# Measured durations in the planner of a fused attention, routing and two-layer kernel, and four buffers for an output tile

## The chip, the cores and the metric

The kernel runs on one core of one Trainium2 chip. The metric is the device time of one execution in microseconds; three runs of the kernel before gave 895.02 (median), 894.41 and 896.03.

## The reference

Three parts follow each other, all in float32:

```python
# 1: retention-like attention, 4 batches x 8 heads x 576 positions x 64
scores = q @ k.T / sqrt(64)
x = (scores * Dmat) @ v            # Dmat[i, j] = gamma_h ** (i - j) for i >= j, else 0
x = x.transpose(0, 2, 1, 3).reshape(2304, 512)
# 2: tokens to 8 experts, at most 2304 / 8 = 288 each, greedily by logit
order = argsort(-(x @ w_gate).flatten())
for idx in order:                  # the highest (token, expert) pair first
    tok, e = idx // 8, idx % 8
    if assigned[tok] >= 0 or counts[e] >= 288: continue
    assigned[tok] = e; counts[e] += 1
out[mask_e] = relu(x[mask_e] @ w1[e]) @ w2[e]     # 512 -> 1024 -> 512
# 3: a dense layer, 512 -> 2048 -> 512
h = out @ w_in;  g = h * tanh(softplus(h));  y = g @ w_out
```

The weights w_in and w_out arrive as 64-bit floats and are narrowed to 32 bits on the chip.

## The kernel before, in words

`attention` computes part 1 tile by tile (18 tiles of 128 tokens). It writes x to a scratch tensor in HBM and keeps the logits. In the same loop 17 of the 32 pieces of w_in and w_out are narrowed (`EARLY = 17`); this is the early narrowing of the kernel. It fills about the first 118 us.

Everything after that is a set of Python generators, started in `moe` (line 877). Each `yield` names an engine, a cost in nanoseconds, the events it comes after, and a priority (lower goes first). `run_tasks` (line 694) is a list scheduler: it holds a planned time per engine, adds 200 ns (`HOP`) for each event, picks the task that can start first (a more urgent one of the same engine goes before it when it could start soon enough), advances the engine's planned time by the cost, and lets the generator emit its instructions. The order of emission is the order of each engine's queue on the chip. The costs are never part of the program: they set only that order. On the chip every engine works off its queue strictly in order and waits for semaphores, so an instruction planned too early holds up all that is behind it.

The generators are these:

- `route` (line 403) finds one expert after the other that fills up: eight rounds. A round takes six steps by a digit of the threshold: VectorE compares (tile G), TensorE counts with 18 small matmuls (pF), VectorE compares the counts (sat), TensorE spreads the digit (pD). Then VectorE marks the tokens (over, scan) and TensorE makes prefix sums (pP). Its priority is 0.
- `tokens` (line 598, priority -1) makes the list of 288 tokens of a group: VectorE compares positions in two halves (ohb), TensorE sums (pI), VectorE makes idx, POOL issues three indirect DMAs which gather rows of x into xg (three of 96 rows of 2 KB), and twelve transposes on TensorE (mmx, line 661) turn them. ScalarE and VectorE split the result into a high and a low float32r part (xh, xl).
- `weights_of` and `unit` load the eight 512 KB units of an expert's weights through SyncE into three stage buffers (st). `split_unit` (line 580) splits each into high and low parts: ScalarE makes whi, POOL or VectorE makes wlo.
- `experts` (line 797, priority 2) runs the products of the experts: per expert 96 matmuls for the first layer (mma, line 784) and 96 for the second (mmb), three for each exact product (high-high, low-high, high-low). ScalarE and VectorE make hh and hl from mma, and ScalarE copies mmb to y, which SyncE stores to HBM. Five PSUM banks go round among mma, mmb, mmx and pI.
- `narrow` (line 732) takes the remaining 15 pieces of w_in and w_out: ScalarE, VectorE (dw, lines 756 and 763) and POOL or VectorE, priority 4, or 1.5 when it falls behind a pace in planned time.
- `tiles` runs the last layer: 96 hidden tiles (mmc), each with a gate of reciprocals and products on VectorE, ScalarE and POOL, and the outer products (po). It begins when the last expert's first layer is done.

The function `result` (line 814) makes y. It asks for the event of the second last store, since there are two buffers:

```python
at = yield ACT, 290, [at, *self.stored[-2:-1]], 0
y = self.fa.tile([P, CAP], F32, name="y", bufs=2)
```

Of the kernel before, what the change touches and what calls it, by code (L numbers as in the profile page):

```python
# [7 lines left out]
F32 = mybir.dt.float32  # L8
# [9 lines left out]
P = 128  # L18
# [6 lines left out]
CAP = N // E  # L25
# [9 lines left out]
NRING = 12  # L35
CLOSED = -1.0e37
# [6 lines left out]
GATHER = 2200  # L43
# [9 lines left out]
EID = -2  # L53
# [79 lines left out]
class Kernel:  # L133
# [267 lines left out]
    def route(self):  # L401
# [8 lines left out]
        for i in range(E):  # L410
# [21 lines left out]
            if i:  # L432
                at = yield DVE, 210, [at], 0
                key = self.at("key")
                v.scalar_tensor_tensor(key, self.dead, CLOSED, raw, op0=ALU.mult, op1=ALU.add)
            known = None
            for s in range(6):
                m = WIDTHS[s]
                if s or i:
                    at = yield DVE, m * 20 + (0, 950, 420, 420, 420, 420)[s], [at], 0  # L440
# [20 lines left out]
                    if s:  # L461
                        side = yield DVE, 300, [at], 0
# [11 lines left out]
                    at = yield PE, 475, [at], 0  # L474
# [3 lines left out]
                    at = yield DVE, 75, [at], 0  # L478
                    sat = self.saturated(pF, m)
                at = yield PE, 20, [at], 0  # L480
                pD = self.psum("pD", [P, E])
                nc.tensor.matmul(pD, self.digit[:m, s, :], sat[:m], start=True, stop=True)
            at = yield DVE, 1400, [at], 0
# [20 lines left out]
            marked = yield PE, 60, [at], 0  # L504
# [12 lines left out]
            at = yield DVE, 900, [marked, at], 0  # L517
# [30 lines left out]
    def weights_of(self, junk, at):  # L548
# [5 lines left out]
        at = yield DVE, 80, [at], EID  # L554
# [24 lines left out]
    def split_unit(self, n, st, at, eng, into, prio):  # L579
# [7 lines left out]
        hi = yield ACT, 950, [at, *before, *place], prio  # L587
# [3 lines left out]
        lo = yield ({POOL: 2310, DVE: 1140} if eng is None else eng), 1140, [hi], prio  # L591
# [4 lines left out]
    def tokens(self, i, pos, at):  # L596
# [4 lines left out]
        at = yield DVE, 600, [at], pr  # L601
# [6 lines left out]
        side = yield DVE, 500, [at], pr  # L608
# [8 lines left out]
        for ts in halves:  # L617
            ready.append((yield DVE, 525, [at], pr))
            v.tensor_tensor(ohb[:, ts], bb[:, ts, None].to_broadcast([P, NT // 2, GB]), self.rc[:, None, RC["slot"]].to_broadcast([P, NT // 2, GB]), op=ALU.is_equal)  # L619
        pI = None  # L620
        for ts, made in zip(halves, ready):
            at = yield PE, 490, [made, side, *([] if pI is not None else [self.bank])], pr
            if pI is None:
                nI, pI = self.take_bank(f"pI{i}")
                pI = pI[:GB, :6]
            for t in range(ts.start, ts.stop):
                nc.tensor.matmul(pI, ohb[:, t], R[:, t].rearrange("p g c -> p (g c)"), start=(t == 0), stop=(t == NT - 1))
        at = yield DVE, 75, [at], pr
# [3 lines left out]
        self.banks[nI] = at  # L632
        if i > 1:
            yield None, 0, [lambda: self.gathered.get(i - 2)], pr
        at = yield POOL, 3100, [at], pr
# [13 lines left out]
        def rest(c, n, pT, at):  # L649
            hi = yield ACT, 290, [at], pr  # L650
            nc.scalar.copy(xh[:, c], pT[:, :CAP])
            ready = yield DVE, 370, [hi], pr
# [32 lines left out]
    def free(self, n):  # L685

        last = [self.banks[j - 5] if len(self.banks) >= 5 - j else Event(0) for j in range(n)]
        return None if None in last else max(last, key=lambda e: e.t)

# [42 lines left out]
    def narrow(self):  # L732
# [16 lines left out]
        def piece(n, st, now, dst):  # L749
            now = yield ACT, 520, [now, *at("turn", n - 1), *at("sign", n - 2)], self.narrow_priority  # L750
# [3 lines left out]
            now = yield DVE, 400, [now, *at("shift", n - 1), *at("store", n - 3)], self.narrow_priority  # L754
# [3 lines left out]
            sign = yield ACT, 520, [now], self.narrow_priority  # L758
            nc.scalar.sign(t, st[:, :, 1].bitcast(F32))
            for c in range(0, 512, 512 // PARTS):  # L760
                cs = slice(c, c + 512 // PARTS)
                now = yield DVE, 665 if PARTS == 1 else 365, [now], self.narrow_priority
                v.scalar_tensor_tensor(w[:, cs], st[:, cs, 0], ic[:, IC["low"]], w[:, cs], op0=ALU.logical_shift_right, op1=ALU.bitwise_or)
            done["read"][n] = max(sign, now, key=lambda e: e.t)
            now = yield {POOL: 1230, DVE: 600}, 0, [now, sign], self.narrow_priority
# [10 lines left out]
    def product(self, name, terms, first=True, last=True, bank=None):  # L776

        n = len(terms)
        for j, term in enumerate(terms):
            for h in range(3):  # L780
                at = yield PE, 123, [lambda: (term() or (0, None))[1], *([] if bank else [self.bank])], 2
# [15 lines left out]
    def experts(self):  # L797
        nc, a = self.nc, self.a
        for i in range(E):
# [3 lines left out]
            def rest(f, bank, at):  # L803
                hi = yield ACT, 290, [at], 0
# [3 lines left out]
                ready = yield DVE, 370, [hi], 2  # L808
# [5 lines left out]
            def result(i, d, bank, at):  # L814
                at = yield ACT, 290, [at, *self.stored[-2:-1]], 0
                y = self.fa.tile([P, CAP], F32, name="y", bufs=2)
# [60 lines left out]
    def moe(self):  # L877
# [15 lines left out]
        self.freed, self.banks, self.stored, self.narrowed = [], [], [], {}  # L893
        self.loaded, self.rounded, self.staged = {}, {}, {}
        self.layer1, self.gathered, self.features = {}, {}, {}
# [213 lines left out]
```

## Time and profile before

| what | us |
|---|---|
| median of three runs | 895.02 |
| the profiled execution | 903.27 |
| its span, first to last instruction | 901.5 |
| TensorE busy | 818.8 (91%) |
| VectorE busy | 699.5 (78%) |
| ScalarE busy | 411.4 (46%) |
| POOL busy | 464.4 (52%) |
| mean granted TensorE clock | 0.933 |

The profile comes from one execution on the chip. A busy time is the sum over the stretches in which the engine executed something. The granted clock is 1.0 when TensorE runs at 2.4 GHz and 0.5 when it runs at 1.2 GHz. A wait is put down to the instruction whose semaphore came last. In the timeline, the bracket behind a row is the idle time of the engine before that row and what ended it.

### The profile page before, as it was taken

The page shows a single profiled execution, that of the slowest core. Times are in us where ns is not written, and L with a number is a line of the kernel's source. Part 1 is how long each engine was busy: PE and PEld are TensorE (multiplying, and loading weights), DVE is VectorE, ACT ScalarE, POOL GpSimd, SP SyncE. Part 2 cuts the span into 40 slices and gives each one's busy share as a digit, 9 for nine tenths or more (in the row PEclk, how much of TensorE's full clock was granted, in tenths as well). Part 3 has the DMA queues.
Part 4 walks back from the last instruction along what each step waited for, and adds up shares of the span by engine and source line. Part 5 has one row for each costly group of instructions (what it writes and reads, how often), then busy time and mean ns, then how long its engine had stood idle before and what let it go on. Part 6 is the DMA issues. An engine that isn't in the chain of part 4 may idle for free.

```text
span 901.5 us, 15523 instructions
## 1 busy us (share of the span) xinstructions
PE 818.8 (91%) x5821; PEld 736.1 (82%) x5821; DVE 699.5 (78%) x1110; ACT 411.4 (46%) x736; POOL 464.4 (52%) x400
## 2 busy tenths in 40 slices
PE   7899864989898989877999988999999999999997
PEld 5788742878787878767999977998999899899995
DVE  4367665687576757766538999999899899899894
ACT  0244421434243434343538544655655655645543
POOL 4466401565655747531003765766655655755644
PEclk9899858788987988988999999999999999999999
DMA  9999736376756768576558010100100100100000
GB/s 345 346 372 371 226 138 143 118 141 213 165 161 160 194 160 160 175 200 169 166 161 270 32 36 1 53 19 0 53 19 1 54 18 1 59 12 1 36 1 36
DMA packets 66331, 112.37 MB, mean 125 GB/s; under 512 B 10192, under 2 KB 38224, under 8 KB 66256
## 3 DMA queue, kind: packets, MB, share of 16 engines
q1 hardware_dynamic: 63280, 101.94, 36.5%
q0 software_dynamic: 2976, 9.44, 5.1%
q8 instruction: 46, 0.75, 0.4%
q14 instruction: 29, 0.24, 0.1%
HBM read 88.81 MB, written 22.55 MB: 124 GB/s over the span
## 4 chain that ended last, share of the span: by engine, by line
PE 51%; DVE 24%; DMA 15%; issue 5%; POOL 3%; ACT 2%; SPq 0%; POOLq 0%; DVEq 0%; ACTq 0%
PE mmc L988 15%; PE po L1049 15%; PE mmb L784 6%; DVE q L1018 5%; DMA xg<-x_scratch,idx 5%; PE mma L784 4%; DVE n L1013 3%; DMA st<-w 2%; PE pF L477 2%; DMA w_out<-dw 2%; DVE ohb L619 2%; DMA st<-w_in 2%; DMA mask<-masks 2%; PE pL L244 2%; PE pA L203 1%
## 5 line engine op out<-in xcount | busy, mean ns | idle before, releaser
L1018 DVE RECIPROCAL q<-q 128x384 f32<-128x384 f32 x96 | 244.1, 2543 | 11.6 <-ACT q L1016 10.5
L592 POOL TENSOR_TENSOR wlo<-st,whi 128x1024 fp32r<-128x1024 f32 x50 | 120.2, 2416 | 153.2 <-ACT whi L589 141.4
L1020 POOL TENSOR_TENSOR n<-n,q 128x384 f32<-128x384 f32 x96 | 99.9, 1040 | 106.4 <-DVE q L1018 102.2
L988 PE MATMUL mmc<-yl,whi 128*128 128x384 f32 x384 | 130.2, 339 | 3.4 <-POOL yl L948 2.9
L988 PE MATMUL mmc<-yh,whi 128*128 128x384 f32 x384 | 130.0, 339 | 2.6 <-DVE n L1023 2.6
L1030 POOL TENSOR_TENSOR gl<-n,gh 128x384 fp32r<-128x384 f32 x96 | 107.4, 1119 | 47.5 <-ACT gh L1028 47.1
L988 PE MATMUL mmc<-yh,wlo 128*128 128x384 f32 x384 | 130.2, 339 | 0.0
L1049 PE MATMUL po<-whi,gl 128*128 128x512 f32 x288 | 114.2, 397 | 0.0
L1049 PE MATMUL po<-wlo,gh 128*128 128x512 f32 x288 | 114.2, 397 | 0.0
L1049 PE MATMUL po<-whi,gh 128*128 128x512 f32 x288 | 112.7, 391 | 0.0
L1013 DVE SCALAR_TENSOR_TENSOR n<-s 128x384 f32<-128x384 f32 x96 | 108.4, 1130 | 0.5
L1006 ACT ACTIVATE s<-mmc 128x384 f32<-128x384 f32 x96 | 47.1, 491 | 120.6 <-PE mmc L988 110.1
L589 ACT CAST whi<-st 128x1024 fp32r<-128x1024 f32 x80 | 83.2, 1045 | 30.3 <-DMA st<-w 24.3
L784 PE MATMUL mmb<-hh,whi 128*128 128x288 f32 x256 | 82.4, 322 | 4.8 <-ACT y L817 4.0
L784 PE MATMUL mmb<-hl,whi 128*128 128x288 f32 x256 | 82.3, 321 | 1.0 <-DVE hl L810 1.0
L784 PE MATMUL mma<-xh,whi 128*128 128x288 f32 x256 | 82.1, 321 | 0.0
L784 PE MATMUL mmb<-hh,wlo 128*128 128x288 f32 x256 | 81.8, 320 | 0.0
L784 PE MATMUL mma<-xh,wlo 128*128 128x288 f32 x256 | 81.0, 316 | 0.0
L784 PE MATMUL mma<-xl,whi 128*128 128x288 f32 x256 | 80.0, 313 | 0.0
L988 PEld LDWEIGHTS mmc<-yl,whi 128*128 128x128 f32 x384 | 72.5, 189 | 8.5 <-POOL yl L948 3.8
L988 PEld LDWEIGHTS mmc<-yh,whi 128*128 128x128 f32 x384 | 72.4, 189 | 7.2 <-DVE n L1023 3.1
L988 PEld LDWEIGHTS mmc<-yh,wlo 128*128 128x128 f32 x384 | 72.6, 189 | 0.0
(155 smaller groups left out, 1641.4 us busy)
## 6 DMA issues: line engine op xcount, KB each, us to landing
st<-w SPq DMA_DIRECT2D x64, 512.0 KB, 4.8
qk<-qk SPq DMA_DIRECT2D x18, 512.0 KB, 7.7
kv<-kv SPq DMA_DIRECT2D x18, 512.0 KB, 7.4
std<-w_in SPq DMA_DIRECT2D x16, 512.0 KB, 4.7
std<-w_out SPq DMA_DIRECT2D x16, 512.0 KB, 5.3
x_scratch<-xs SPq DMA_DIRECT2D x18, 256.0 KB, 3.4
y_scratch<-y SPq DMA_DIRECT2D x32, 144.0 KB, 3.2
yt<-y_scratch SPq DMA_DIRECT2D x22, 192.0 KB, 2.7
```

The source lines that it names most:

```text
L244: nc.tensor.matmul(pL, XT[t][:, c, :], wgt[:, c, :], start=(c == 0), stop=(c == HP - 1))
L477: nc.tensor.matmul(pF[:m, :], G[:, t, :m], oh[:, t, :], start=(t == 0), stop=(t == NT - 1))
L589: self.nc.scalar.copy(dst[0], st)
L592: (self.nc.vector if lo.engine == DVE else self.nc.gpsimd).tensor_tensor(dst[1], st, dst[0].bitcast(F32), op=ALU.subtract)
L784: self.nc.tensor.matmul(bank[1][:, :CAP], al if h == 2 else ah, bl if h == 1 else bh, start=(first and j == h == 0), stop=(last and j == n ...
L988: self.nc.tensor.matmul(bank[1][:, :TILE], (wl if h == 2 else wh)[:, c, cs], x[c][h == 1], start=(c == h == 0), stop=(c == HP - 1 and h == 2))
L1006: nc.scalar.activation(s, p, AF.Sigmoid)
L1013: v.scalar_tensor_tensor(u, s, 2.0, s, op0=ALU.subtract, op1=ALU.mult)
L1018: v.reciprocal(q, q)
L1020: nc.gpsimd.tensor_tensor(u, u, q, op=ALU.mult)
L1030: nc.gpsimd.tensor_tensor(gl, u, gh.bitcast(F32), op=ALU.subtract)
L1049: nc.tensor.matmul(po[j], (gl if h == 2 else gh)[:, js], (wl if h == 1 else wh)[:, f % 2], start=(f == h == 0), stop=(f == DFF // P - 1 an ...
```

## The change

Three things change. First, some thirty costs that the generators yield are replaced by longer ones, in routing, token lists, weight splits, narrowing and expert products; the costs of the last layer stay. Second, the tile y gets four buffers instead of two, and the copy into y comes after the store four tiles back, counted by a new function `y_place`. Third, the list of a group is planned only behind the list of the group before it (`self.listed`). The instructions themselves and their number stay as they are.

```diff
+YB = 4
-GATHER = 2200
+GATHER = 7500
 # route
-                at = yield DVE, 210, [at], 0
+                at = yield DVE, 180, [at], 0
-                    at = yield DVE, m * 20 + (0, 950, 420, 420, 420, 420)[s], [at], 0
+                    at = yield DVE, m * 21 + (10, 970, 500, 500, 500, 500)[s], [at], 0
-                        side = yield DVE, 300, [at], 0
+                        side = yield DVE, 340, [at], 0
-                    at = yield PE, 475, [at], 0
+                    at = yield PE, 80 + 15 * m, [at], 0
-                    at = yield DVE, 75, [at], 0
+                    at = yield DVE, 155, [at], 0
-                at = yield PE, 20, [at], 0
+                at = yield PE, 105, [at], 0
-            at = yield DVE, 1400, [at], 0
+            at = yield DVE, 2100, [at], 0
-            marked = yield PE, 60, [at], 0
+            marked = yield PE, 190, [at], 0
-            at = yield DVE, 900, [marked, at], 0
+            at = yield DVE, 1600, [marked, at], 0
 # weights_of, split_unit
-        at = yield DVE, 80, [at], EID
+        at = yield DVE, 160, [at], EID
-        hi = yield ACT, 950, [at, *before, *place], prio
+        hi = yield ACT, 1060, [at, *before, *place], prio
-        lo = yield ({POOL: 2310, DVE: 1140} if eng is None else eng), 1140, [hi], prio
+        lo = yield ({POOL: 2480, DVE: 1240} if eng is None else eng), 1240, [hi], prio
 # tokens
-        at = yield DVE, 600, [at], pr
+        at = yield DVE, 600, [at, *([lambda: self.listed.get(i - 1)] if i else [])], pr
-        side = yield DVE, 500, [at], pr
+        side = yield DVE, 700, [at], pr
-            ready.append((yield DVE, 525, [at], pr))
+            ready.append((yield DVE, 1050, [at], pr))
-            at = yield PE, 490, [made, side, *([] if pI is not None else [self.bank])], pr
+            at = yield PE, 740, [made, side, *([] if pI is not None else [self.bank])], pr
-        at = yield DVE, 75, [at], pr
+        at = yield DVE, 160, [at], pr
-        self.banks[nI] = at
+        self.banks[nI] = self.listed[i] = at
-        at = yield POOL, 3100, [at], pr
+        at = yield POOL, 3700, [at], pr
-            hi = yield ACT, 290, [at], pr           # xh
+            hi = yield ACT, 420, [at], pr
-            ready = yield DVE, 370, [hi], pr        # xl
+            ready = yield DVE, 455, [hi], pr
 # narrow
-            now = yield ACT, 520, ...               # dt, twice
+            now = yield ACT, 680, ...
-            now = yield DVE, 400, ...               # dw, line 756
+            now = yield DVE, 860, ...
-                now = yield DVE, 665 if PARTS == 1 else 365, ...   # dw, line 763
+                now = yield DVE, 1060, ...
-            now = yield {POOL: 1230, DVE: 600}, 0, ...
+            now = yield {POOL: 1310, DVE: 690}, 0, ...
 # product, experts
-                at = yield PE, 123, ...
+                at = yield PE, 132, ...
-                hi = yield ACT, 290, [at], 0        # hh
+                hi = yield ACT, 420, [at], 0
-                ready = yield DVE, 370, [hi], 2     # hl
+                ready = yield DVE, 455, [hi], 2
-                at = yield ACT, 290, [at, *self.stored[-2:-1]], 0
-                y = self.fa.tile([P, CAP], F32, name="y", bufs=2)
+                at = yield ACT, 410, [at, self.y_place], 0
+                self.made += 1
+                y = self.fa.tile([P, CAP], F32, name="y", bufs=YB)
+    def y_place(self):
+        n = self.made - YB
+        return Event(0) if n < 0 else self.stored[n] if n < len(self.stored) else None
```

## Rows read from the trace of the kernel before

**Rows 1.** Busy by stretch: PE, PEld, DVE, ACT, POOL (xcount), clock, DMA share, GB/s.
```profile
160.00:425.00 265.00, 227.53 (x1970) 208.28 (x1970) 187.38 (x546) 103.91 (x175) 147.53 (x80) 0.88 0.67 169
425.00:492.00 67.00, 66.47 (x485) 66.05 (x484) 37.60 (x50) 36.47 (x61) 5.61 (x3) 1.00 0.61 196
492.00:620.00 128.00, 122.52 (x598) 110.15 (x598) 124.66 (x93) 69.96 (x136) 84.15 (x75) 0.97 0.10 32
620.00:880.00 260.00, 260.00 (x1305) 235.57 (x1305) 248.10 (x189) 145.03 (x273) 154.48 (x161) 1.00 0.07 22
```

**Rows 2.** Waits of TensorE from 160 to 425: us, times, longest.
```profile
PE mmx L661 <- DMA xg<-x_scratch,idx: 11.4, 6, 3.7
PE mmx L661 <- DVE hl L810: 4.3, 1, 4.3
PE mmb L784 <- ACT y L817: 4.0, 1, 4.0
PE pD L482 <- DVE sat L398: 3.6, 1, 3.6
PE pF L477 <- DVE G L459: 3.5, 4, 1.0
PE pI L627 <- DVE ohb L619: 3.5, 10, 0.8
PE mmx L661 <- issue: 2.0, 1, 2.0
PE pP L506 <- DVE scan L503: 1.8, 1, 1.8
...
```

**Rows 3.** Timeline of TensorE from 248.2: start, us, engine, line, tiles, [idle before].
```profile
248.25 0.40 PE L784 MATMUL mmb<-hh,whi 128*128 128x288 f32 x1 [4.02 <-ACT y L817]
248.49 0.30 PE L784 MATMUL mmb<-hl,whi 128*128 128x288 f32 x1
248.62 0.29 PE L784 MATMUL mmb<-hh,wlo 128*128 128x288 f32 x1
...
248.92 0.44 PE L784 MATMUL mmb<-hl,whi 128*128 128x288 f32 x1
249.16 0.44 PE L784 MATMUL mmb<-hh,wlo 128*128 128x288 f32 x1
```

**Rows 4.** Tile xg, then timeline of TensorE at the seventh gather's transposes.
```profile
DMA to landing us min/median/max: 4.6/10.2/13.2
...
396.00 0.42 PE L661 MATMUL mmx<-cst,xg 96*128 96x96 f32 x1 [3.72 <-DMA xg<-x_scratch,idx]
398.40 1.86 PE L661 MATMUL mmx<-cst,xg 96*128 96x96 f32 x10 [1.99 <-DMA xg<-x_scratch,idx]
```

**Rows 5.** Chain that ended last, in order of time: start, us, what.
```profile
393.22 19.07 DMA st<-w
...
412.32 1.04 ACT whi L589
```

**Rows 6.** Timeline of TensorE: the second gather's transposes, the second expert's first product.
```profile
202.98 1.70 PE L661 MATMUL mmx<-cst,xg 96*128 96x96 f32 x10
...
206.81 0.40 PE L784 MATMUL mma<-xh,whi 128*128 128x288 f32 x1
```

**Rows 7.** Groups of VectorE, 160 to 425: busy us, mean ns, idle before.
```profile
L756 DVE TENSOR_SCALAR dw<-dt,ic 128x512 uint32<-128x512 uint32 x13 | 20.7, 1596 | 0.0
L763 DVE SCALAR_TENSOR_TENSOR dw<-std,ic,dw 128x512 uint32<-128x512 uint32 x13 | 19.4, 1495 | 0.0
L619 DVE TENSOR_TENSOR ohb<-sc,rc 128x864 bf16<-128x864 f32 x14 | 14.1, 1047 | 0.0
```

**Rows 8.** The chain that ended last, at a store of y.
```profile
237.82 9.88 DMA y_scratch<-y
```

**Rows 9.** Timelines of VectorE and POOL from 193.
```profile
194.07 6.57 DVE L756 TENSOR_SCALAR dw<-dt,ic 128x512 uint32<-128x512 uint32 x1
...
193.35 6.99 POOL L592 TENSOR_TENSOR wlo<-st,whi 128x1024 fp32r<-128x1024 f32 x3
```

More of the change, by code (lines that the diff above doesn't have):

```diff
@@ L749, in piece @@
         def piece(n, st, now, dst):
-            now = yield ACT, 520, [now, *at("turn", n - 1), *at("sign", n - 2)], self.narrow_priority
+            now = yield ACT, 680, [now, *at("turn", n - 1), *at("sign", n - 2)], self.narrow_priority
             t = self.conv.tile([P, 512], F32, name="dt", bufs=2)
@@ L753, in piece @@
             done["turn"][n] = now
-            now = yield DVE, 400, [now, *at("shift", n - 1), *at("store", n - 3)], self.narrow_priority
+            now = yield DVE, 860, [now, *at("shift", n - 1), *at("store", n - 3)], self.narrow_priority
             w = self.conv.tile([P, 512], U32, name="dw", bufs=3)
@@ L757, in piece @@
             done["shift"][n] = now
-            sign = yield ACT, 520, [now], self.narrow_priority
+            sign = yield ACT, 680, [now], self.narrow_priority
             nc.scalar.sign(t, st[:, :, 1].bitcast(F32))
@@ L761, in piece @@
                 cs = slice(c, c + 512 // PARTS)
-                now = yield DVE, 665 if PARTS == 1 else 365, [now], self.narrow_priority
+                now = yield DVE, 1060, [now], self.narrow_priority
                 v.scalar_tensor_tensor(w[:, cs], st[:, cs, 0], ic[:, IC["low"]], w[:, cs], op0=ALU.logical_shift_right, op1=ALU.bitwise_or)
             done["read"][n] = max(sign, now, key=lambda e: e.t)
-            now = yield {POOL: 1230, DVE: 600}, 0, [now, sign], self.narrow_priority
+            now = yield {POOL: 1310, DVE: 690}, 0, [now, sign], self.narrow_priority
             w = w.bitcast(F32)
@@ L780, in product @@
             for h in range(3):
-                at = yield PE, 123, [lambda: (term() or (0, None))[1], *([] if bank else [self.bank])], 2
+                at = yield PE, 132, [lambda: (term() or (0, None))[1], *([] if bank else [self.bank])], 2
                 bank = bank or self.take_bank(name)
@@ L892, in moe @@
         self.weights, self.final = [], {}
-        self.freed, self.banks, self.stored, self.narrowed = [], [], [], {}
+        self.freed, self.banks, self.stored, self.narrowed, self.made = [], [], [], {}, 0
         self.loaded, self.rounded, self.staged = {}, {}, {}
-        self.layer1, self.gathered, self.features = {}, {}, {}
+        self.listed, self.layer1, self.gathered, self.features = {}, {}, {}, {}
         self.sent, self.ahead = [], []
```

## The prediction, made before the result was known

> **What bounds the kernel now.** The view of busy time by stretch comes first, since the kernel is a row of stages with different limits [rows 1]. In the last two stretches, from 492 us on, TensorE is busy 122.52 of 128 us and 260.00 of 260 us. VectorE is nearly as full beside it, with 124.66 of 128 and 248.10 of 260. No cost of that layer is edited and nothing in it can shrink by reordering, so I treat it as a block that starts when the expert stage lets it. From 425 to 492 TensorE is busy 66.47 of 67 us at the full clock: by then a backlog of expert products has built up. What is left is 160 to 425 us, the stage in which routing, gathers, expert products, weight loads and narrowing are interleaved by the planner. There TensorE is busy 227.53 of 265 us, so it idles 37.5 us, at a mean granted clock of 0.88.
>
> As the engine has work waiting in nearly all of that stage, an idle microsecond there is mostly one in which the next instruction of its in-order queue was not ready while a later one was. The second view is therefore the list of what TensorE waited for in that stretch [rows 2]. It holds thirty waits and about 37 us. The transposes of gathered tokens lead with 11.4 us behind the gather's DMA and 2.0 us more noted as issue. Then come 4.3 us behind VectorE's hl, 4.0 us behind ScalarE's copy of y, 3.6 and 3.5 us inside the routing steps, 3.5 us for the token lists (pI behind ohb) and 1.8 us for the routing's prefix sums (pP behind scan).
>
> Third, the timeline around one such wait [rows 3] shows its second price. Before and just behind the 4.02 us wait the matmuls start 0.13 us apart (248.49 to 248.62). From 248.92 they start 0.24 us apart, which is the lower of the clock's two levels. A mean of 0.88 puts 24% of 265 us, 64 us, on that level. Had TensorE computed through all of it, it would have lost 32 us. Against 37.5 us of idling that is at most 0.85 us of clock for each us of wait. I take 0.5, because part of the low clock lies inside the waits themselves.
>
> **The change part by part.** No instruction is added or removed. The planner's costs move, and with them the places in each engine's queue, and y gets four buffers.
>
> *Gathers (cost 2200 to 7500 behind a POOL slot of 3100 to 3700, idx 75 to 160).* The twelve transposes of a group come 5300 + 600 + 85 ns = 6.0 us later in the plan, with expert matmuls pulled in front of them. On the chip a gather takes 10.2 us from issue to landing in the median, 13.2 at most [rows 4], so the old plan was about 8 us short and the new one about 3. The waits at the transposes are 11.4 + 2.0 = 13.4 us. Of these 3.72 + 1.99 = 5.7 us belong to the seventh gather [rows 4], which leaves 7.7 us for the earlier ones, each wait 1 to 4.4 us long. A shift of 6.0 us covers every one. I book 7.7 us, and with the clock (half as much again, here and below) 11.6 us. For the seventh I book nothing: right behind it ScalarE's whi sits at the head of its queue until 412.32 for a weight load that was 19.07 us under way [rows 5], hh and hl queue behind that, and TensorE waits the 4.3 us of [rows 2]. If TensorE comes there 5.7 us sooner it waits 5.7 us longer. The upper bound is 5.7 us and its clock, 10 us. The second gather is the one with little slack: its transposes start at 202.98 and its first product at 206.81 [rows 6]. If they move 6.0 us, the product can start late by what is left of 3.8 us of slack after the 1.8 us of transposing, so 0 to 4 us are lost. I take 2.
>
> *Token lists (ohb 525 to 1050 per half, pI 490 to 740).* Measured is 1047 ns [rows 7]; the old plan sent TensorE to pI a microsecond early in every round. I book the whole 3.5 us, with the clock 5.2. The bounds are 0 and 6.5.
>
> *The routing's end (1400 to 2100, 900 to 1600).* TensorE gets some five more expert matmuls ahead of pP. The 1.8 us wait goes, with the clock 2.7.
>
> *Four places for y, and y_place.* A store of y was 9.88 us under way beside a gather [rows 8]. Copy and store of the result two tiles later had to wait for it, and TensorE behind them lacked a bank for 4.02 us [rows 3]. With four places the copy would need the store of four tiles earlier, so the wait goes: 4.0 us, with the clock 6.0. Its cover if it fails is none; the 4.0 us would stay. SyncE's queue holds the same stores, only issued sooner, in front of weight loads that wait for the splits anyway.
>
> *Narrowing (400 to 860, 665 to 1060, ScalarE's 520 to 680).* Here a single number can't be right. Of dw on line 756 the mean is 1596 ns, on line 763 it is 1495 ns [rows 7], and one took 6.57 us, from 194.07 to 200.64, while POOL ran three splits in a row from 193.35 to 200.34 [rows 9]. The Trainium skill (SBUF — State Buffer, section Who interferes with whom) says that a VectorE instruction in a two-port mode and a GpSimd instruction block each other for the whole of whichever started first. By it these meetings stay, however the plan is costed, and the sum gets nothing here. By the new costs taken at their word the thirteen and thirteen would take 25.0 us, not 20.7 + 19.4 = 40.1. The trace agrees with the rule. Either way I book zero. The bounds are 15 us of VectorE gained or as much again lost, of which TensorE saw 3.6 + 3.5 us [rows 2].
>
> *The rest (hh, hl, xh, xl, splits, product 123 to 132, the wait on the list before).* They stretch the plan by a few per cent where the queue already ran that slow. The added wait (a group's list only behind the list before it) holds back VectorE's first list instructions of the later group; behind them in its queue stand the same lists and, in the last rounds, splits of weights, and TensorE's pI waits for them. The lists share one ohb buffer already, so it orders what had to be in that order. I book zero for these edits themselves.
>
> *New stalls.* A queue that is dealt again meets other late operands. The nearest rows are the two kinds of wait that no edit addresses, 3.6 and 3.5 us [rows 2]. I let the new order add as much again, 7.1 us. The bounds are 0 and 15.
>
> Sum: 11.6 + 5.2 + 2.7 + 6.0 - 2 - 7.1 = 16.4, so 16 us. (The waits alone are 7.7 + 3.5 + 1.8 + 4.0 = 17.0.) The profiled execution of 903.27 us (span 901.5) would become 887. It lies 8.25 us above the median of the runs, 895.02, and I take the difference off that: 879 us.
>
> **The rivals.**
> *Given back before the last layer.* The weights, not TensorE, close the stage: the load that landed at 412.3 [rows 5] had gathers for the last two groups beside it, and a sooner routing brings those together all the same. Then only what shortens the routing itself comes through. I put that at y and half of pP and pI, 4.0 + 0.9 + 1.7 = 6.6 us, less 2 for the second gather: about 4.6 us, 890 us. For it speaks that VectorE feels the same DMA through whi; against it, that TensorE works from 425 to 492 without a gap [rows 1], so it has products in hand there that a sooner start would simply move.
>
> *Slower: narrowing meets POOL's splits inside the routing steps.* The place is VectorE between pF and pD, the price up to 6.57 - 0.86 = 5.7 us above the new cost for a meeting, as at 194.07 [rows 9]. Their excess over the new costs is now 40.1 - 25.0 = 15 us. If the new order brings two thirds more such meetings into the steps and half of the booked 25.5 us fails, then 895 - 12.7 + 2 + 10 of blocked routing + 7.1 of new stalls is 901 us. It decides from the point at which the last gather is issued later than now. By the rule of the Trainium skill cited above (SBUF — State Buffer, section Who interferes with whom) each meeting is such a block; the trace shows them, at [rows 9].
>
> *The order hardly changes.* The longer costs stretch all queues alike, and transposes and lists keep their neighbours: 895 us. Against it, the gather's cost grows by a factor of 3.4 while the product's grows by 7%.
>
> **How the numbers follow.** Forecast 0.56; given back 0.21; slower 0.16; no change 0.07. Faster by more than 0.2% (about 1.8 us, what a measurement here can tell from no change) is the first two: 0.77; within 0.2% it is 0.07; slower 0.16. The forecast's own range comes from its bounds: with 0.85 us of clock per us, the seventh gather and no new stalls it is 17.0 x 1.85 + 10 - 2 = 39 us; with no clock and 15 us of new stalls it is 17.0 - 4 - 15 = -2 us. Both ends together are unlikely, so the low end is 864. At the top it takes in the case of the gain given back, no change and a little of the slower one: 897.
>
> **What would show each step right or wrong.** Waits of mmx for the gather near 2 us or less up to the sixth gather, pI behind ohb near zero, no wait of mmb behind ScalarE's y, and none of pP behind scan; a granted clock above 0.88 in the stage, 0.92 or so; the stretch of full TensorE and VectorE that now starts at 492 us starting some 16 us sooner, and lasting as long as now. The dw of 2 to 6 us should still be there beside POOL's splits. The forecast is wrong if TensorE idles as much as now in other places, if the last layer waits for its weights, or if the last gather is issued no sooner.

## The result: slower, not faster

| runs | kernel before | changed kernel | ratio, 95% interval |
|---|---|---|---|
| four of each, on the chip of the times above | 895.52 us (894.41 to 899.06) | 905.99 us (904.03 to 909.81) | 1.0115 [1.0071, 1.0159] |
| again, on another chip (`e17_after_again`) | 907.62 us (16 runs) | 911.21 us (12 runs) | 1.0057 [1.0025, 1.0090] |

The forecast was 879 us, which is 1.8% faster. The kernel is 0.6 to 1.2% slower, 3.6 to 10.5 us by the two pairs of medians.

The profiled execution took 906.62 us (span 904.8). Lines behind the edits are one to seven higher: L790 is the old L784, L662 the old L661, L816 the old L810. The kernels differ in one thing that "The instructions themselves and their number stay as they are" leaves out: the planner also chooses between POOL and VectorE by their costs, for the low part of a split (wlo) and for the last product of a narrowing piece. With the new costs four splits and three such products went from VectorE to POOL (54 of the 80 splits run there, before 50). By stretch, with the columns of [rows 1] and one stretch more at the end:

```profile
160.00:425.00 265.00, 219.89 (x1966) 205.60 (x1964) 190.47 (x526) 100.66 (x168) 148.49 (x81) 0.89 0.62 165
...
492.00:620.00 128.00, 118.84 (x586) 106.78 (x585) 125.55 (x94) 68.61 (x134) 83.61 (x75) 0.98 0.10 32
...
612.00:622.00 10.00, 5.30 (x20) 4.19 (x19) 9.22 (x9) 4.89 (x10) 7.47 (x7) 0.82 0.00 1
```

From 160 to 425 TensorE computes 219.89 us against 227.53 [rows 1], so it idles 45 us and not 37.5, at much the same clock (0.89, 0.88). What it waited for, from 157 to 456, to set beside [rows 2]:

```profile
PE pF L478 <- DVE known L465: 13.3, 6, 3.5
PE pI L628 <- DVE hl L816: 11.1, 5, 3.3
PE mmx L662 <- DVE xl L654: 9.7, 1, 9.7
PE pD L483 <- DVE sat L399: 7.8, 5, 4.5
PE pI L628 <- DVE ohb L620: 2.1, 2, 1.7
PE mmb L790 <- ACT y L824: 1.2, 1, 1.2
```

Hardly a row of [rows 2] is left. The 13.4 us at the gathers are gone, and so are pP's 1.8 us and hl's 4.3 us; y has 1.2 us of 4.0, ohb 2.1 of 3.5. In their place stand waits that the kernel before had little of or not at all: known 13.3 us, pI behind hl 11.1, xl 9.7 and 4.2 more behind sat.

How far such a list repeats shows in a second profiled execution of either kernel over the same stretch, first the kernel before (`e1`), then the changed one (`e17`):

```profile
PE mmx L661 <- DMA xg<-x_scratch,idx: 19.4, 9, 6.1
PE mmx L661 <- DVE hl L810: 7.1, 1, 7.1
...
PE pI L627 <- DVE ohb L619: 3.3, 9, 0.8
...
PE mmb L784 <- ACT y L817: 1.9, 1, 1.9
```

```profile
PE pI L628 <- DVE hl L816: 10.9, 5, 3.1
PE pF L478 <- DVE known L465: 8.4, 4, 2.9
PE pD L483 <- DVE sat L399: 8.1, 5, 4.8
PE mmx L662 <- DVE xl L654: 5.1, 1, 5.1
```

Which waits a kernel has repeats: gathers and hl before, pI behind hl, known, sat and xl after. Their size does not: the gathers cost the same kernel 11.4 and 19.4 us, y 4.0 and 1.9. A term booked from one trace, and a difference between two single traces further below, can be off by as much.

Where a span goes can be cut at four instructions: the first product of the first expert, the first product of the last expert (the expert stage ends there), the first hidden tile of the last layer, and the 49th hidden tile. Their starts in the profiled executions, two for each kernel, give:

| profiled execution | start | expert stage | to first hidden tile | to 49th tile | rest | span |
|---|---|---|---|---|---|---|
| before | 159.7 | 297.9 | 19.2 | 207.3 | 217.5 | 901.5 |
| before again (`e1`) | 161.8 | 305.1 | 20.1 | 207.3 | 217.5 | 911.8 |
| after | 157.3 | 299.1 | 19.1 | 211.8 | 217.5 | 904.8 |
| after again (`e17`) | 157.3 | 295.1 | 19.1 | 210.2 | 217.5 | 899.2 |

Two things are to be seen. In the expert stage, where 16 us were booked, the two pairs disagree: the changed kernel is 1.2 us longer in the first and 10.0 us shorter in the second, while two executions of one kernel differ there by 7.2 and 4.0 us. TensorE idled 37.5 and 40.8 us in this stage before, 45.9 and 37.1 after: it idles about as much as it did, in other places. And the last layer, which I had called a block that cannot change, is 2.9 to 4.5 us longer up to its 49th tile. The profiled executions of the kernel before were 8.3 and 8.9 us above the medians of their kernel on their chips (895.02 and 905.11) and those of the changed kernel 0.6 us above and 10.2 below, so these four rows show less of the loss than the medians do. If that excess lies in the expert stage, where most of the scatter is, the stage takes an estimated 290 and 296 us before and 299 and 305 us after at the medians, some 9 us more; no profiled execution shows that directly.

### The profile page after: what moved, and what is told of

It reads as the page before. It is cut to its first block, busy times and chain, and to the rows that moved or that the text cites. A ratio compares the mean times of both kernels' runs of the same rounds, so it can differ in the third digit from the quotient of the medians.

```text
span 904.8 us, 15533 instructions
## 1 busy us (share of the span) xinstructions
PE 819.0 (91%) x5835; PEld 737.4 (82%) x5835; DVE 703.1 (78%) x1103; ACT 410.5 (45%) x736; POOL 478.4 (53%) x407
## 4 chain that ended last, share of the span: by engine, by line
PE 52%; DVE 28%; DMA 12%; issue 3%; POOL 2%; ACT 2%; SPq 0%; POOLq 0%; DVEq 0%; ACTq 0%
PE mmc L995 15%; PE po L1056 15%; PE mmb L790 8%; DVE q L1025 8%; PE mma L790 6%; DVE n L1020 4%; DVE dw L762 3%; PE pF L478 2%; DVE dw L769 2%; DMA st<-w 2%; DMA w_out<-dw 2%; DMA std<-w_out 2%; DMA mask<-masks 2%; DVE G L460 1%; DMA kv<-kv 1%
## 5 line engine op out<-in xcount | busy, mean ns | idle before, releaser
L1025 DVE RECIPROCAL q<-q 128x384 f32<-128x384 f32 x96 | 244.2, 2544 | 11.1 <-ACT q L1023 9.4
L593 POOL TENSOR_TENSOR wlo<-st,whi 128x1024 fp32r<-128x1024 f32 x54 | 128.7, 2403 | 165.7 <-ACT whi L590 154.5
L1020 DVE SCALAR_TENSOR_TENSOR n<-s 128x384 f32<-128x384 f32 x96 | 106.3, 1109 | 3.5 <-ACT s L1013 2.7
L790 PE MATMUL mmb<-hh,whi 128*128 128x288 f32 x256 | 83.0, 324 | 1.2 <-ACT y L824 1.2
L790 PE MATMUL mmb<-hh,wlo 128*128 128x288 f32 x256 | 82.5, 322 | 0.0
L790 PE MATMUL mmb<-hl,whi 128*128 128x288 f32 x256 | 82.3, 321 | 0.0
L790 PE MATMUL mma<-xh,whi 128*128 128x288 f32 x256 | 81.0, 316 | 0.0
L790 PE MATMUL mma<-xh,wlo 128*128 128x288 f32 x256 | 80.5, 314 | 0.0
L790 PE MATMUL mma<-xl,whi 128*128 128x288 f32 x256 | 78.9, 308 | 0.0
```

The source lines that it names most:

```text
L593: (self.nc.vector if lo.engine == DVE else self.nc.gpsimd).tensor_tensor(dst[1], st, dst[0].bitcast(F32), op=ALU.subtract)
L790: self.nc.tensor.matmul(bank[1][:, :CAP], al if h == 2 else ah, bl if h == 1 else bh, start=(first and j == h == 0), stop=(last and j == n ...
L1020: v.scalar_tensor_tensor(u, s, 2.0, s, op0=ALU.subtract, op1=ALU.mult)
L1025: v.reciprocal(q, q)
```

## The experiments

Each edit is to the kernel named, and each ratio is to the kernel before on the same chip. The letters in the quoted expectations name theories; the text says in words what became of each.

**The kernel before, unedited, and three parts of the change alone.**

```diff
 # e2: before           # e3: after            # e4: before
-GATHER = 2200         -GATHER = 7500         -y: two buffers, stored[-2:-1]
+GATHER = 7500         +GATHER = 2200         +y: YB = 4, y_place
```

> The kernel before, unchanged, for a second profile of it: its profiled execution lay 8 us above the median of its runs, so a trace nearer to 895 us is wanted. Theory A (the new order puts narrowing and late list instructions into the routing steps; the cost is in the expert stage): the ratio is 1.000 within 0.4%, and in this trace the last layer's first gates start some 7 us sooner than at 484 us. Theory B (the new order loses in the last layer, at the boundary between its second and third token tile): the expert stage stands as in the first profile and the last layer is 8 us shorter.

> The kernel before with GATHER 7500 alone. Theory A: transposes no longer wait (11.4 us of waits for the gather fall below 3), the routing steps are not touched, so it is faster, 885 to 893 us. Rival (the gather's cost is what delays, as every group's features come later): 900 us or more, with the last gather issued later than 394 us.

> The changed kernel with GATHER back at 2200. Theory A: the narrowing and list stalls stay and the waits of the transposes come back, so it is as slow as the changed kernel or slower, 905 to 915 us. Rival (the gather's cost is what delays): back near 895 us.

> The kernel before with four places for y alone. Theory A: the 4.0 us wait of mmb behind y goes and nothing else changes, 889 to 895 us. Rival (the places are what costs, through stores issued sooner in SyncE's queue): 900 us or more.

Measured: e1 0.9998 [0.9954, 1.0043] (its runs go from 902.0 to 915.3 us); e2 0.9886 [0.9815, 0.9957]; e3 1.0254 [1.0189, 1.0318]; e4 1.0007 [0.9969, 1.0045]. Neither theory about e1 came out: its profiled execution lay above its median again, with the last layer as long as in the first profile. The gather's cost is worth 1.1% alone and 1.4 to 1.9% within the change (1.0115 and 1.0057 against e3's 1.0254; e3 is slower than either of its theories expected), so the direction of that step was right here; `e16` below shows another base on which the same edit loses. In e2 the waits at the gathers are gone, yet TensorE idled 38.3 us in the expert stage, as much as before. Other waits have taken their place, 10.2 us of the transposes behind hl the largest, and the stage is shorter (290.3 us) because TensorE was busy 252.1 us and not 260.4 for the same products. The four places are worth nothing alone, where 6.0 us were booked. The wait of mmb behind y is gone in e4's trace. Its waits behind hl and ohb are 5.7 and 5.4 us for 4.3 and 3.5 [rows 2], but as e1 has 7.1 and 3.3 of these, it is not shown that TensorE merely came to them sooner.

**Which of the other costs lose.** The changed kernel with one group of costs back at the old numbers:

```diff
 # e5: narrow            # e6: all nine of route       # e9: only the marks
-ACT 680, DVE 860, 1060  (the steps and the marks)     -2100, 190, 1600
+ACT 520, DVE 400, 665                                 +1400, 60, 900
 # e10: only the steps                                        # e13: the splits
-m * 21 + (10, 970, 500, ...), 340, 80 + 15 * m, 155, 105     -1060, 2480, 1240
+m * 20 + (0, 950, 420, ...), 300, 475, 75, 20                +950, 2310, 1140
```

> The changed kernel with the five costs of the narrowing pieces back at their old values. Theory A (the narrowing's VectorE work now stands inside the routing steps and is blocked there by POOL's splits) in its form that these costs put it there: ratio to before 0.985 to 0.998, the rounds of the routing back to some 40 us from 42. Theory A2 (other costs put it there): still 1.005 to 1.015 with rounds of 42 us and about 53 us of dw on VectorE.

> The changed kernel with the nine costs inside the routing generator back at their old values. If the longer planned routing steps are what lets narrowing and late list work in: ratio to before 0.985 to 0.998. If not: 1.005 to 1.015, and the waits of pF behind known and of pI behind hl stand as in the changed kernel (13.3 and 11.1 us).

> The changed kernel with three routing costs back: the marking (2100 to 1400), the prefix sums (190 to 60), the closing of a round (1600 to 900). Theory C (longer planned routing puts more expert matmuls into TensorE's queue in front of each routing instruction, so that the routing, whose end releases the last groups, comes later): in the queue 979 expert matmuls stand in front of the routing's last prefix sum, 1032 in the changed kernel, 948 before, 879 with all routing costs back. Ratio to before about 1.000, between 1.0115 and 0.9916. Theory D (the placing of VectorE's work in a round decides, not the count): either near 0.99 or near 1.01, by which of the two halves carries it.

> The changed kernel with the other routing costs back, those of the six steps (compare, count, sat, digit). 987 expert matmuls stand in front of the last prefix sum. Theory C: about 1.002. Theory D: the opposite of the run before.

> The changed kernel with the costs of the weight splits back (ScalarE 1060 to 950, POOL and VectorE 2480/1240 to 2310/1140). Theory L (these costs, which the last layer's weights use too, shift the last layer's queues so that TensorE waits for yl at the third token tile): the waits of mmc behind POOL's yl fall from 4.7 us to about 1, and from the first hidden tile to the 49th it takes 207 to 208 us instead of 211.8. If only that changed, the ratio would be 1.007. Rival: other costs do it, 211 to 212 us.

Measured: e5 1.0021 [0.9979, 1.0062]; e6 0.9916 [0.9886, 0.9946]; e9 0.9987 [0.9954, 1.0019]; e10 0.9857 [0.9799, 0.9915]; e13 0.9979 [0.9945, 1.0012]. Every one of them lies below the changed kernel's 1.0057 to 1.0115. e5 fell between its two theories. The steps are the dearest: with those five costs back the kernel is 2.0 to 2.6% faster than with them. Its waits and stretches:

```profile
PE pF L478 <- DVE known L465: 10.3, 5, 4.6
PE mmx L662 <- DMA xg<-x_scratch,idx: 5.0, 4, 1.8
PE pD L483 <- DVE sat L399: 3.2, 3, 1.5
...
160.00:425.00 265.00, 239.35 (x2141) 224.29 (x2141) 195.08 (x551) 113.48 (x193) 152.49 (x82) 0.92 0.70 182
```

TensorE computes 239.35 of 265 us there, 19 us more than in the changed kernel. The pI waits behind hl and the long xl wait are not among them. The rounds of routing take 36.0 to 40.2 us from one to the next (41.1 to 43.6 in the changed kernel; 39.1 to 40.4 before, and 47.8 for the first), and the last gather is issued at 385.4 us and not 409.0. These lines are of an execution of 881.27 us, the fastest of e10's six, 8 us under their median of 889.19. e6, which has these five back and four more, is at 0.9916, above e10 but with an interval that overlaps e10's, so what the five are worth beside other costs stays open. The splits that went to POOL are not the loss by themselves: the two fastest kernels below, e12 and e18, have 54 of them there too.

**Is it VectorE blocked beside POOL?** This is the slower rival (theory A in the expectations). Both kernels got narrowing instructions on VectorE with 16 of the 512 columns, one operand in PSUM; the queues' order is that of their parents, and the narrowed weights are not computed.

```diff
 # e7: after, e8: before (the second instruction, L769 and L763, in the same way)
-v.tensor_scalar(w, t.bitcast(U32), ic[:, IC["three"]], None, op0=ALU.logical_shift_left)
+v.scalar_tensor_tensor(w[:, :16], self.at("ic", U32)[:, :16], ic[:, IC["low"]],
+                       t[:, :16].bitcast(U32), op0=ALU.logical_shift_right, op1=ALU.bitwise_or)
```

> The changed kernel, its plan and queues the same, but each narrowing piece does on VectorE only two operations of 16 columns that take one input from PSUM, and POOL multiplies the signs alone (the narrowed weights are not computed). Theory A (blocked narrowing is the loss): it gains 2% or more on the changed kernel and falls below the same edit of the kernel before by about 1% (the gathers' gain). Rival (the order of the other work is itself worse): it stays some 1% above the same edit of the kernel before.

> The kernel before with the same short narrowing, plan and queues the same (the narrowed weights are not computed). Theory A: 0.985 to 0.995 of before, since its narrowing is blocked less often. Rival: the same, but below the changed kernel with this edit.

Measured: e7 1.0103 [1.0068, 1.0137], e8 0.9955 [0.9918, 0.9992]. The blocked narrowing is there in the changed kernel, worse than before. First its groups on VectorE from 160 to 425 (columns as in [rows 7]), then VectorE at two of them and POOL beside the first:

```profile
L762 DVE TENSOR_SCALAR dw<-dt,ic 128x512 uint32<-128x512 uint32 x13 | 27.9, 2144 | 0.0
L769 DVE SCALAR_TENSOR_TENSOR dw<-std,ic,dw 128x512 uint32<-128x512 uint32 x14 | 25.6, 1831 | 0.0
...
188.99 9.03 DVE L769 SCALAR_TENSOR_TENSOR dw<-std,ic,dw 128x512 uint32<-128x512 uint32 x1
197.95 0.15 DVE L399 TENSOR_SCALAR sat<-pF 63x8 bf16<-63x8 f32 x1
...
276.18 4.60 DVE L762 TENSOR_SCALAR dw<-dt,ic 128x512 uint32<-128x512 uint32 x1
280.71 0.16 DVE L444 TENSOR_REDUCE sc<-pD 128x1 uint32<-128x8 f32 x1
...
189.26 6.99 POOL L593 TENSOR_TENSOR wlo<-st,whi 128x1024 fp32r<-128x1024 f32 x3
196.22 1.25 POOL L773 TENSOR_TENSOR dw<-dw,dt 128x512 f32<-128x512 f32 x1
```

The same instruction takes 9.03 us here and 0.75 us at 185.23, and sat behind it cost TensorE 4.52 us at 198.15; the second cost it 2.84 us at known. Narrowing is 53.5 us of VectorE and not 40.1 [rows 7] (46.2 and 34.0 in the second executions). With it cut to 6.0 us, though, the changed kernel is no faster. Its waits:

```profile
PE pI L628 <- DVE hl L816: 10.9, 5, 3.1
PE mmx L662 <- DVE xl L654: 10.1, 1, 10.1
PE mmx L662 <- DMA xg<-x_scratch,idx: 9.0, 8, 4.4
PE mmx L662 <- ACT y L824: 8.8, 3, 4.0
PE pD L483 <- DVE sat L399: 5.1, 2, 4.0
```

The waits at known fell from 13.3 to 1.5 us, and the gathers, which had none, have 9.0 us, and mmx behind y 8.8. The rival was right about the place and about its sign (the last gather is issued at 409 us in both executions, not at 394 and 399), and it isn't the cause: without blocked narrowing the rounds from the second on still take 44.3 us on average, the total stays, and the waits stand elsewhere in the same order.

**Is it pI behind hl?** (Theory P.) Five times TensorE stands up to 3.3 us in front of pI, although ohb has been made. The timelines at one of them, VectorE and then TensorE:

```profile
263.43 2.02 DVE L620 TENSOR_TENSOR ohb<-sc,rc 128x864 bf16<-128x864 f32 x2
265.36 1.33 DVE L460 TENSOR_TENSOR G<-sc,rc 128x1134 bf16<-128x1134 f32 x1
266.61 1.91 DVE L816 SCALAR_TENSOR_TENSOR hl<-mma,hh 128x288 fp32r<-128x288 f32 x5
...
267.11 0.93 PE L628 MATMUL pI<-R,ohb 128*96 128x6 bf16 x18 [1.80 <-DVE hl L816]
```

pI takes the PSUM bank of a first-layer product, which comes free with that product's hl, and five hl stand in VectorE's queue behind ohb and G. Two kernels take the wait away: pI in a bank of the routing (e14, same queues), and hl at an urgent priority (e15).

```diff
 # e14: after                                        # e15: after
-nI, pI = self.take_bank(f"pI{i}")                   -ready = yield DVE, 455, [hi], 2    # hl
+pI = self.psum("pI", [P, 512])    # bank rB         +ready = yield DVE, 455, [hi], -2
```

> The changed kernel with pI in a PSUM bank of the routing instead of one of the five of the products; plan and queues of all engines are the same, instruction for instruction. Theory P (pI waits for a bank that VectorE's hl frees, and hl stands behind the lists): the 11.1 us of pI behind hl go, ratio 1.000 to 1.006. Rival (the expert matmuls behind pI need the same banks, so the wait moves to them): the same sum of waits under mma, ratio 1.008 to 1.015.

> The changed kernel with hl planned ahead of the lists (priority -2 instead of 2). Theory P: from hh to hl it takes 1.5 us in the mean instead of 3.0, no wait of pI behind hl, ratio 0.985 to 1.003. Rival (hl only takes VectorE's time from the routing): 1.005 to 1.02, with rounds longer than 42 us.

Measured: e14 1.0076 [1.0040, 1.0112], e15 1.0157 [1.0090, 1.0223]. The first waits of e14, then of e15:

```profile
PE pD L483 <- DVE sat L399: 13.0, 6, 4.8
PE mmx L663 <- DVE xl L655: 11.8, 1, 11.8
PE pF L478 <- DVE known L465: 8.6, 4, 2.7
```

```profile
PE mma L790 <- ACT xh L652: 23.5, 4, 12.9
PE pD L483 <- DVE sat L399: 17.5, 9, 5.5
...
```

Both are rid of the 11.1 us, neither is faster than the changed kernel. In e14, with each queue as it was, TensorE idled 42.6 us in the expert stage, between the changed kernel's 45.9 and 37.1. Sat has 13.0 us there where the two executions of the changed kernel have 7.8 and 8.1, xl 11.8 where they have 9.7 and 5.1: most of what went is waited for at other places. pI shares its new bank with pD and pP, and waits 2.3 us for a read of pP.

**How close the plan's product cost may be to the chip's.** From [rows 3] a product starts every 0.13 us at the full clock and every 0.24 us at the low one; the plan says 123 ns before and 132 after.

```diff
 # e11: after      # e12: before      # e16: before
-PE, 132           -PE, 123           -PE, 123, GATHER = 2200
+PE, 155           +PE, 105           +PE, 105, GATHER = 7500
```

> The changed kernel with the cost of an expert matmul at 155 instead of 132, all other costs as changed: 887 expert matmuls stand in front of the routing's last prefix sum instead of 1032. Theory C: as fast as with the routing costs back, ratio 0.985 to 0.998, rounds of 38 us, the last gather issued at 380 to 390 us. Theory D (the long routing costs are bad in themselves): 1.005 to 1.015.

> The kernel before with the cost of an expert matmul at 105 instead of 123: 1079 expert matmuls stand in front of the routing's last prefix sum instead of 948. Theory C: slower than before, ratio 1.01 to 1.02, rounds of 43 us or more, the last gather issued after 405 us. Theory D: 0.995 to 1.005.

> The kernel before with the expert matmul at 105 and GATHER at 7500. If the two gains (0.9778 and 0.9886) come from different waits and add: 0.962 to 0.972. If the gain of the first is one favourable order among many, which the second deals again: 0.975 to 1.00.

Measured: e11 0.9958 [0.9922, 0.9993]; e12 0.9778 [0.9716, 0.9841] at 883.24 us (881.36 to 886.99), faster than both kernels; e16 1.0064 [1.0027, 1.0102]. That a longer first part of the rounds, more products in front of the routing's end, is worse (theory C) falls with e12, which has more of them than either kernel: 1079 ahead of the last pP in TensorE's queue, against 948 before and 1032 after. The 0.9778 was expected by neither theory. And two edits that gain alone, 2.2% and 1.1%, lose 0.6% together, beyond either expectation of e16. The first waits of e12, a stretch of it, and the first waits of e16:

```profile
PE pD L482 <- DVE sat L398: 12.3, 11, 4.2
PE mmx L661 <- DMA xg<-x_scratch,idx: 10.5, 4, 5.7
...
160.00:425.00 265.00, 237.07 (x2137) 221.73 (x2136) 191.23 (x558) 110.18 (x190) 149.54 (x81) 0.92 0.65 174
```

```profile
PE mma L784 <- ACT xh L651: 17.4, 3, 6.6
PE pF L477 <- DVE G L459: 14.9, 5, 4.8
...
```

e12 still waits 10.5 us for gathers, which the change set out to remove. But it has few other waits: TensorE idled 27.9 us in the expert stage, at a granted clock of 0.92 from 160 to 425 where it was 0.88 [rows 1]. That was luck: no theory aimed at this order.

**The last layer, and how large the loss is.** Two runs close what was left open: the changed kernel again (in the table at the top), and both the steps' and the splits' costs back.

> The changed kernel once more, unedited, on another chip. The ratio 1.0115 stands on four runs of either kernel on one chip, where the kernel before ran at 895.5 us; in the later studies the kernel before ran at 904 to 907. Theory N (the loss is the changed order's, 4.5 us in the last layer and the rest in the expert stage): 1.007 to 1.016 again, the changed kernel at 911 to 920. Theory U (the loss is in part that the kernel before was quick on that one chip; the pair of profiles shows a difference of 3.4 us, all of it in the last layer): 1.000 to 1.005, the changed kernel at 904 to 910.

> The changed kernel with the five costs of the routing steps (m * 20 ..., 300, 475, 75, 20) and the three costs of the splits (950, 2310, 1140) back at the old numbers; gathers, lists, narrowing, products and the four places stay changed. If the losses are two separate blocks (steps in the expert stage, splits in the last layer): the steps alone gave 0.9857, and the last layer goes from 211 to 204 us, so 0.975 to 0.981, and the expert stage stays at about 273 us. If every edit of a cost deals the whole order again: the expert stage is another, 285 to 305 us, and the ratio 0.985 to 1.01.

e17's ratio, 1.0057, lies between what N and U expected, with an interval that reaches into both, and the 3.6 us between its medians are little more than the last layer's 2.9 us in its trace. e18 measured 0.9826 [0.9775, 0.9876].

TensorE and POOL of the changed kernel, where the extra time of the last layer lies, and then POOL of the kernel before at the same tile:

```profile
615.32 0.45 PE L995 MATMUL mmc<-yl,whi 128*128 128x384 f32 x1 [1.50 <-POOL yl L955]
619.31 0.69 PE L995 MATMUL mmc<-yl,whi 128*128 128x384 f32 x1 [3.20 <-POOL yl L955]
...
616.05 0.99 POOL L1027 TENSOR_TENSOR n<-n,q 128x384 f32<-128x384 f32 x1 [0.79 <-DVE q L1025]
617.00 1.31 POOL L1037 TENSOR_TENSOR gl<-n,gh 128x384 fp32r<-128x384 f32 x1
618.27 0.99 POOL L955 TENSOR_TENSOR yl<-yt,yh 128x384 fp32r<-128x384 f32 x1
...
617.30 1.31 POOL L948 TENSOR_TENSOR yl<-yt,yh 128x384 fp32r<-128x384 f32 x1
618.57 1.02 POOL L1030 TENSOR_TENSOR gl<-n,gh 128x384 fp32r<-128x384 f32 x1
```

The next tokens' yl, which TensorE needs, stands in POOL's queue behind gl of another tile; in the kernel before it stands in front of that gl. TensorE waits 4.7 us where it waited 0.6, and at 619.31 a matmul takes 0.69 us that takes 0.34 at 612.59; the clock is 0.82 from 612 to 622. From the 33rd to the 49th tile that is 74.9 us against 67.8 before. In the twenty traces of this case this swap and the time go together without exception: with yl behind gl the stretch takes 74.4 to 75.1 us (both executions of the changed kernel, e3, e5, e6, e7, e9, e10, e14, e16), with yl in front 67.2 to 68.2 us (both of the kernel before, e2, e4, e8, e11, e12, e13, e15, e18).

So this part of the loss is one pair of neighbours in POOL's queue that changed places. It is not the splits' longer costs as such (theory L): e13 and e18, with those costs back, have the good order, but so have e11 and e15, which keep the longer ones, and e16, with the old ones, has the bad order. The tiles ahead of the swap went 2.6 and 4.2 us quicker in the changed kernel (136.9 and 135.3 us for the first 32, before 139.5 in both executions), so of the 7.1 us 4.5 and 2.9 are left at the 49th tile.

Whether the gains of e10 and of the splits add in e18 is not settled. Its last layer gained 4.9 us on e10's, its expert stage is 286.0 us against 272.9, but e10's trace is the fastest of its six runs, and e18's 0.9826 lies between the two expectations, with an interval that reaches into both.

## Why the prediction was wrong

The step that failed is "New stalls. ... I let the new order add as much again, 7.1 us" (its bounds were 0 and 15), and with it "I book zero for these edits themselves". Counted in the expert stage of the first pair of traces, TensorE idled 37.5 us before and 45.9 after. What left: 13.4 us at gathers, 4.3 + 1.7 behind hl, 2.8 of y, 1.8 of pP, 2.8 of G, 1.4 of ohb and 0.3 of eid, 28.5 us in all. What came: pI behind hl 11.1, known 12.0 more, xl 9.7, sat 4.2 more, 37.0 us in all. In e17 29 us came. So it came to four or five times the stalls booked, and to at least as much as had left. Two of the prediction's own signs of being wrong came true with it: TensorE idles as much as before in other places, and the last gather is issued no sooner.

Two readings led there. The prediction called the waits behind sat and G, 3.6 and 3.5 us, "the two kinds of wait that no edit addresses", but five of the edited costs are those of just these routing steps, and no term of the sum stands for them; with them back, e10 is 2.0 to 2.6% faster. And it said of the last layer "No cost of that layer is edited", but `split_unit` also splits the last layer's weights, 16 of the 80 units, and the order there changed too. The sum also charged the clock (half as much again) for the waits that go and not for the 2 and 7.1 us that come; charged for all it is 1.5 x (17.0 - 2 - 7.1) = 12 us and not 16. Point by point:

- *Gathers*, 7.7 us of waits booked: the waits went as said, those of the seventh too. What they are worth hangs on the order: e2 and e3 show 1.1% and more, and on e12's costs the same edit lost 2.9% (e16 against e12). The last gather's landing (median 9.7 us, 10.2 before [rows 4]) has not changed.
- *Seventh gather*, zero booked since the weights end later: right in kind. ScalarE's whi waited for a load again, as in [rows 5], and TensorE 9.69 us at the last transposes. The chain of waits there:

```profile
408.04 15.85 DMA st<-w
...
423.92 1.04 ACT whi L590
424.96 0.31 ACT xh L652
...
425.29 0.47 DVE xl L654
```

- *Second gather*, 2 us lost: the shift came, the loss did not. Its transposes start at 205.52 and its expert's first product at 208.94, 2.1 us later than in [rows 6], but TensorE works on mmb until then and has no wait there.
- *Token lists*, 3.5 us: the ohb waits fell to 2.1, but TensorE now waits 13.2 us in front of pI, 11.1 of them because the bank came free later than the list.
- *The routing's end*, 1.8 us: pP's wait went. But all rounds from the second on became longer, 42.5 us on average and not 39.6 (42.4 and 40.8 in the second executions), and from the last round's mark to its gather it is 25.8 us and not 17.8. So the last gather is issued at 409.0 us, 15 us later than before (408.7 and 399.4 in the second executions). I had only asked what leaves TensorE's list, not how long a round becomes.
- *Four places*, 4.0 us: the wait fell to 1.2, and e4 shows that it was worth nothing. In e1 it was only 1.9 us to begin with.
- *Narrowing*, zero: dw became 13.4 us longer, near the upper bound of 15, and e7 shows that the total didn't follow it. The Trainium skill (SBUF — State Buffer, section Who interferes with whom) says that when VectorE and GpSimd want the same pair of SBUF ports, the second to issue blocks until the first has finished. The 9.03 us above are such a block, and one that lasted over four instructions of POOL in a row.
- *The last layer as a block*: wrong by 2.9 to 4.5 us, by the swap in POOL's queue.

Of the rivals, the slower one came nearest in time (901) and in its mark, and its mechanism fell with e7. "The order hardly changes" was off by its reason. My chance of 0.16 for slower was too low because I treated the stalls of a new order as a small correction to the stalls of the old one. They are as large as each other: the old order was one in which 37 us of waits were left, and a new order draws its own (25.6 to 58.6 us of idling in the expert stage over the orders tried, each from one trace).

What stays open: by medians up to 10.5 us were lost, of which the traces place 2.9 to 4.5 in the last layer. The expert stage of two profiled executions of either kernel (297.9 and 305.1, 299.1 and 295.1) doesn't show the rest. Nor is it settled why one order has fewer late operands than another; no single cost explains it, and e2, e12 and e16 show that the effects of two costs don't add.

## What to carry to other kernels

In a list-scheduled kernel with in-order queues a truer cost is not a gain in itself: the waits that it removes are real, but the whole order is dealt again, so book as many new stalls as the stage has now, and make the range as wide as the orders are. Here fifteen orders of the same work lay between 0.978 and 1.025 of the kernel before. Try several costs and measure them, and look past the stage edited: who stands in front of the needed operand in each queue, also in stages whose costs nobody touched.

## What the runs showed of the hardware that was not expected

- A VectorE dw (L769) that took 0.75 us at 185.23 took 9.03 us while POOL ran three splits and a product one after the other (189.26 to 197.47); here the meeting lasted as long as POOL's run of ready work, not as long as one instruction.
- A load of 512 KB of weights took 15.85 us beside the gathers of the last rounds, and 19.07 in [rows 5].
- The same kernel varies more between executions than the first three runs told: the kernel before ran from 894.4 to 899.1 us on one chip and from 902.0 to 915.3 us in the ten runs of e1, with medians of 895.5 on the first chip and 904 to 908 on the others, and most of the difference between two profiled executions lay in the expert stage.
